# A gated Fourier and squared-ReLU mix in split float32: h as the transposed product, x's operands of three products from DRAM, and one more second-level product

## The chip, the cores and the metric

The kernel runs on one core of one Trainium2 chip. The metric is the device time of one execution in microseconds (us); of several runs the median is taken. The profile is a separate, profiled execution of the same program; it has a span (first to last instruction on the core) and a device time of its own.

## The reference, cut to what matters

```python
a = jnp.einsum("bsd,ed->bse", x, dft_hid_re)          # x is [2048, 1024]
b = jnp.einsum("bsd,ed->bse", x, dft_hid_im)
y = jnp.einsum("ts,bse->bte", dft_seq_re, a) - jnp.einsum("ts,bse->bte", dft_seq_im, b)
h = jnp.einsum("bsd,df->bsf", x, w1) + b1             # w1 is [1024, 3584]
r = jnp.where(h > 0, h, 0)
o = jnp.einsum("bsf,fd->bsd", r * r, w2) + b2
g = sigmoid((x * gate_w).sum(-1, keepdims=True))
out = g * y + (1 - g) * o
```

All of it is float32. x enters three times: in a and b, in h, and in the gate.

## The kernel before, in words

**Four stages.** x_stage (line 664) makes "x W", the products a and b, and keeps them in DRAM (`ab`). c_stage (780) makes y times g, kept in DRAM (`gy`). h_stage (683) makes the squared ReLU of h, kept in DRAM (`h_far`), in two parts: part 0 has 2048 of the 3584 features, part 1 the other 1536. o_stage (802) makes the output. On TensorE (PE) the stages stand one after the other, each a list of steps.

**Split float32.** An operand is a block of 128 partitions by 1024 floats. ScalarE (ACT) makes `hi`, its rounding to fp32r (line 220), and VectorE (DVE) makes `lo`, the difference (line 230). A step multiplies two operands by `hi*hi`, `hi*lo` and `lo*hi` (line 306): per 128 output rows six matmuls of 512 columns. A step has `rows` such rows: 4 in x_stage and in the first part of h, 3 in the second part, whose weight operands are 768 floats wide.

**Seven products.** Each stage is cut into 2x2 quarters and multiplied by seven products in place of eight (`seven`, line 366), in the order 1, 2, 5, 6, 3, 7, 4. The factors of a product are quarters, or sums S1 to S4 of left quarters and T1 to T4 of right quarters (lines 33 to 38):

```python
SUMS_L = {"S1": ((1, 0), (1, 1), ADD), "S2": ("S1", (0, 0), SUB), "S3": ((0, 0), (1, 0), SUB),
          "S4": ((0, 1), "S2", SUB)}
FACTORS = {1: ((0, 0), (0, 0)), 2: ((0, 1), (1, 0)), 3: ("S4", (1, 1)), 4: ((1, 1), "T4"), 5: ("S1", "T1"),
           6: ("S2", "T2"), 7: ("S3", "T3")}
```

The sums are DVE work on raw blocks from DRAM (line 172). In `wide` (line 568, for x_stage and h_stage) a product is made in one of two ways. `direct` (line 611) cuts it into 2x2 blocks and takes eight steps; its factors are four left and four right operands. `twice` (line 623) applies the seven products once more to those blocks: seven steps, with seven left and seven right operands and four further sums on each side. Which products go `twice` is in TWICE_X and TWICE_H (lines 20 and 24): x_stage and the first part have 1, 2, 5, 3 and 4, the second part 2, 5, 3 and 4. Products 6 and 7 are direct everywhere.

**Left and right.** In x_stage x is the left matrix (its sums are S1 to S4) and W the right one. In h_stage w1 is the left one and x the right one (sums T1 to T4), so the sums of x that h_stage needs are others than those of x_stage, and x_stage's operands cannot serve again.

**Taking the results up.** A step's result in PSUM goes to SBUF by an ACT copy (`put`, line 596) or a DVE addition (`add`, line 603); product 7 and others start from a value that ACT copies into PSUM (line 293). When a block of h is complete, `final` (line 697) does two Relu with the bias (L700) and one Square (L702) on ACT, and a store to DRAM on GpSimd's (POOL) queue follows. Blocks completed by a DVE addition have their `final` put off by LATER = 3 steps.

**What sets the order.** A planner written out by hand (lines 909 to 966) walks over the steps and, ahead of each, emits loads on SyncE's (SP) queue, then the stores that are due (on POOL's queue), then sums with `hi`, then `lo`. An item is loaded as early as 12 steps ahead if slots are free, its sum and its `hi` are made at least 3 steps ahead, its `lo` at least 2; with time left by the planner's own costs, up to 9. There are 55 slots of one block each. Each engine works through its own list in order. A step is 24 matmuls with 4 rows and 18 with 3.

## Time and profile before

| | us |
|---|---|
| median of 3 runs | 1891.17 (1890.40 to 1892.99) |
| the profiled execution | 1888.96 |
| its span | 1886.9 |

In the profile, busy times are of five engines: PE (matmuls; PEld are its weight loads), DVE, ACT, POOL and SP. `L306` is line 306 of the kernel, `ps<-hi,lo` a matmul into PSUM that reads a `hi` and a `lo`, `raw` a block loaded from DRAM, `sum` a sum of blocks, `h`, `u` and `ab` results and intermediate results. A wait is written as the waiting instruction, an arrow, and what it waited for. Granted clock was 0.999 of full speed. The 8244 matmuls of line 306 are shared out so: x_stage 1224, c_stage 2580, the first part of h 1224, its second part 936, o_stage 2280.

### The profile page before, as it was taken

Reading aid. Unit: us, or ns where it says so; the run is one execution under the profiler, and the core shown is the slowest. Engines: PE = TensorE matmul, PEld = TensorE weight load, DVE = VectorE, ACT = ScalarE, POOL = GpSimd, SP = SyncE. Lnnn points to the kernel's source line nnn. Section 1 sums busy time; section 2 is a strip of 40 time slices with the busy share of each in tenths; the row PEclk is TensorE's granted clock in tenths of the full one; section 3 lists DMA queues with packets and bytes.
Section 4 is the critical chain, followed back from the end, with each engine's and each line's share of the span. In section 5 each row is a group of like instructions: output and inputs, shape, how many; then the busy total and the mean of one; then the engine's idle time right before and its main releaser. Section 6 shows DMA issues by size and latency. Waiting matters only on the chain.

```text
span 1886.9 us, 21962 instructions
## 1 busy us (share of the span) xinstructions
PE 1876.6 (99%) x8288; PEld 1551.3 (82%) x8288; DVE 1610.3 (85%) x1543; ACT 1001.3 (53%) x1123; POOL 86.8 (5%) x161
## 2 busy tenths in 40 slices
PE   9999999999999999999999999999999999999998
PEld 7888888888888888888888888888888888888887
DVE  8997898599777998798896997989976997789882
ACT  6474564363343554455484797767954434264440
POOL 0000110000010000000000000000100001000000
PEclk9999999999999999999999999999999999999999
DMA  5732989339786489383551865628872887629971
GB/s 223 247 121 86 348 288 412 129 117 375 261 312 256 151 322 383 139 312 112 170 198 56 325 228 195 228 84 299 293 259 97 317 336 265 218 103 370 409 300 45
DMA packets 128425, 442.93 MB, mean 235 GB/s; under 512 B 14128, under 2 KB 23616, under 8 KB 128320
## 3 DMA queue, kind: packets, MB, share of 16 engines
q1 hardware_dynamic: 106416, 363.26, 53.0%
q0 software_dynamic: 21472, 77.61, 10.3%
q8 instruction: 65, 1.06, 0.2%
q10 hardware_dynamic: 432, 0.66, 0.1%
q14 instruction: 40, 0.33, 0.1%
HBM read 362.83 MB, written 78.65 MB: 234 GB/s over the span
## 4 chain that ended last, share of the span: by engine, by line
PE 97%; DVE 2%; ACT 0%; DMA 0%; issue 0%; SPq 0%; DVEq 0%; ACTq 0%
PE ps L306 97%; DVE lo L230 1%; DVE h L603 0%; DVE sum L172 0%; DMA raw<-in_w 0%; DVE o L818 0%; ACT u L596 0%; ACT hi L220 0%; DVE o L820 0%; DVE raw L172 0%; SPq L152 0%; DVEq L172 0%; DVEq L230 0%; ACTq L596 0%
## 5 line engine op out<-in xcount | busy, mean ns | idle before, releaser
L306 PE MATMUL ps<-hi 128*128 128x512 f32 x2328 | 905.7, 390 | 4.0 <-ACT hi L220 3.6
L306 PE MATMUL ps<-lo,hi 128*128 128x512 f32 x2328 | 905.3, 389 | 0.0
L306 PE MATMUL ps<-hi,lo 128*128 128x512 f32 x2328 | 904.2, 389 | 0.1
L220 ACT ACTIVATE hi<-raw 128x1024 fp32r<-128x1024 f32 (+2 forms) x413 | 420.6, 1037 | 399.0 <-DVE raw L172 274.1
L230 DVE TENSOR_TENSOR lo<-raw,hi 128x1024 fp32r<-128x1024 f32 (+2 forms) x413 | 484.5, 1199 | 57.5 <-ACT hi L220 31.3
L306 PEld LDWEIGHTS ps<-hi 128*128 128x128 f32 x2328 | 437.2, 188 | 95.9 <-ACT hi L220 4.2
L306 PEld LDWEIGHTS ps<-hi,lo 128*128 128x128 f32 x2328 | 437.1, 188 | 92.0 <-DVE lo L230 1.0
L306 PEld LDWEIGHTS ps<-lo,hi 128*128 128x128 f32 x2328 | 437.3, 188 | 91.0 <-DVE lo L230 0.4
L172 DVE TENSOR_TENSOR raw<-raw 128x1024 f32<-128x1024 f32 (+1 forms) x276 | 326.4, 1207 | 56.4 <-DMA raw<-in_ct 19.4
L220 ACT ACTIVATE hi<-sum 128x1024 fp32r<-128x1024 f32 (+1 forms) x172 | 176.1, 1036 | 184.8 <-DVE sum L172 151.2
L306 PE MATMUL ps<-hi,both 128*128 128x512 f32 x840 | 259.8, 389 | 0.0
L230 DVE TENSOR_TENSOR lo<-sum,hi 128x1024 fp32r<-128x1024 f32 (+1 forms) x172 | 203.3, 1198 | 32.9 <-PE ps L306 16.6
L306 PEld LDWEIGHTS ps<-hi,both 128*128 128x128 f32 x840 | 157.7, 188 | 33.8 <-ACT ps L293 0.7
L306 PE MATMUL ps<-lo,both 128*128 128x512 f32 x420 | 163.5, 389 | 0.0
L172 DVE TENSOR_TENSOR sum<-raw 128x1024 f32<-128x1024 f32 (+1 forms) x116 | 121.9, 1066 | 35.4 <-PE ps L306 28.1
L172 DVE TENSOR_TENSOR sum<-raw,sum 128x1024 f32<-128x1024 f32 (+2 forms) x87 | 96.8, 1119 | 12.0 <-PE ps L306 11.7
L603 DVE TENSOR_TENSOR h<-h,ps 128x1024 f32<-128x1024 f32 x92 | 98.2, 1086 | 9.6 <-ACT u L596 7.1
L596 ACT ACTIVATE u<-ps 128x1024 f32<-128x1024 f32 x76 | 71.9, 950 | 62.0 <-PE ps L306 54.3
L306 PEld LDWEIGHTS ps<-lo,both 128*128 128x128 f32 x420 | 78.8, 188 | 16.1
L293 ACT ACTIVATE ps<-u 128x1024 f32<-128x1024 f32 (+1 forms) x74 | 70.0, 953 | 22.2 <-DVE o L831 12.0
L700 ACT ACTIVATE h<-h,b1c 128x512 f32<-128x512 f32 x112 | 74.3, 712 | 6.3 <-DVE h L603 6.0
L220 ACT ACTIVATE both<-sum 128x512 fp32r<-128x512 f32 x60 | 37.1, 625 | 52.7 <-DVE sum L172 33.4
(61 smaller groups left out, 650.5 us busy)
## 6 DMA issues: line engine op xcount, KB each, us to landing
raw<-in_ct SPq DMA_DIRECT2D x151, 512.0 KB, 6.2
raw<-h SPq DMA_DIRECT2D x132, 512.0 KB, 7.3
raw<-in_x SPq DMA_DIRECT2D x107, 512.0 KB, 5.3
raw<-in_w SPq DMA_DIRECT2D x98, 512.0 KB, 6.3
raw<-ab SPq DMA_DIRECT2D x72, 512.0 KB, 6.8
h<-h POOLq DMA_DIRECT2D x48, 512.0 KB, 5.7
raw<-in_w1a SPq DMA_DIRECT2D x36, 512.0 KB, 5.0
ab<-ab POOLq DMA_DIRECT2D x32, 512.0 KB, 6.7
```

The source lines that it names most:

```text
L172: nc.vector.tensor_tensor(self.slot[:, k, c], src[0][:, k, c], src[1][:, k, c], op=self.op)
L220: nc.scalar.activation(self.hi[:, k, c], self.block.slot[:, k, c], AF.Copy)
L230: nc.vector.tensor_tensor(self.lo[:, k, c], self.block.slot[:, k, c], self.hi[:, k, c].bitcast(F32), op=SUB)
L293: nc.scalar.activation(t[:, :n, :], b.slot[:, at:at + n, :], AF.Copy, scale=self.sign)
L306: nc.tensor.matmul(self.ps[r // self.per][:, r % self.per, :], a[:, kk, r * P:(r + 1) * P], b[:, kk, :], start=self.at == 1 and kk + n == ...
L596: nc.scalar.activation(view(near.slot, k), view(ps, k), AF.Copy, scale=float(sign))
L603: nc.vector.tensor_tensor(view(near.slot, k), view((src or dst)[k].slot, k), view(ps, k), op=ADD if sign > 0 else SUB)
L700: nc.scalar.activation(dst.slot[:, k, :], (dst.slot if ps is None else ps)[:, k, :], AF.Relu, bias=b1c[:, tile0 + k:tile0 + k + 1])
```

## The change

It has three parts.

- **The transposed product in h_stage** (`flip`, FLIP = True). The product of w1 and x is formed as its transpose is: x takes the sums S1 to S4 and the weights take T1 to T4, and the factors of every product change sides (`turn`). The steps on PE keep their form: weights stationary, x moving.
- **x's operands from x_stage by DRAM** (KEEP_X). x's operands of products 6, 3 and 5 are now the same in x_stage and in both parts of h_stage: four of product 6 (direct), seven each of products 3 and 5. x_stage stores their `hi` and `lo` to DRAM after making them (`keep`, 36 stores on POOL's queue). h_stage loads them back as finished operands (`Fetched`: two loads on SP's queue into two slots, with no sum, no `hi` and no `lo` to make). Products 1, 2, 4 and 7 make their operands of x as before.
- **One more product by a second level.** Product 1 of the second part goes `twice`: seven steps of 18 matmuls in place of eight.

FAR_WIDE, which was empty, goes. The listing of the changed program has 8226 matmuls of line 306, 58 fewer tensor-tensor instructions on DVE (1418 for 1476), 26 fewer activations (1095 for 1121), 36 more DMA issues on POOL and 40 more on SP: 72 loads of kept operands, and 32 fewer of x.

```diff
-FAR_TALL, FAR_WIDE = ("T2",), ()
-TWICE_H = (1, 2, 5, 3, 4), (2, 5, 3, 4)
+FAR_TALL = "T2",
+ALL = *range(1, 8), *(("direct", m, q) for m in range(2) for q in range(2))
+KEEP_X, KEEP_H, FLIP = {6: ALL, 3: ALL, 5: ALL}, {}, True
+TWICE_H = (1, 2, 5, 3, 4), (1, 2, 5, 3, 4)
...
+        def keep(self):
+
+            self.far = Kept("hi"), Kept("lo")
+            self.uses += 2
...
             for k, c in self.cuts:
                 nc.scalar.activation(self.hi[:, k, c], self.block.slot[:, k, c], AF.Copy)
                 yield
+            if self.far:
+                stores.append((self.far[0], Copy(self, self.hi.bitcast(F32)), 0, 2))
...
             self.block.used()
+            if self.far:
+                stores.append((self.far[1], Copy(self, self.lo.bitcast(F32)), 0, 2))
...
+    class Copy:
+        def __init__(self, base, slot):
+            self.base, self.slot, self.uses = base, slot, 1
+
+        def used(self):
+            self.base.used()
+
+    class Fetched:
+        def __init__(self, far):
+            self.blocks, self.uses = far, 0
+
+        def room(self):
+            return 2
...
+        def load(self, engines):
+            self.hi, self.lo = take("hi", F32R), take("lo", F32R)
+            for b, t in zip(self.blocks, (self.hi, self.lo)):
+                assert b.done
+                next(engines).dma_start(t.bitcast(F32), b.at)
+
+        def sum(self):
+            return 0.0
+
+        def rest(self):
+            return 0.0
...
+        def turn(a, b):
+            return (b, a) if flip else (a, b)
...
+        def of_x(p, part, make):
+
+            if (p, part) in shared:
+                return Fetched(shared[p, part])
+            o = make()
+            if part in keep.get(p, ()):
+                o.keep()
+                shared[p, part] = o.far
+            return o
...
-            l, r = FACTORS[p]
-            mvs = [[right[q, c].operand(r) for q in range(2)] for c in range(2)]
+            l, r = turn(*FACTORS[p])
+
+            def st(m, q):
+                o = lambda: left[m, q].operand(l, rows * P)
+                return o() if x_right else of_x(p, ("direct", m, q), o)
+
+            def mv(q, c):
+                o = lambda: right[q, c].operand(r)
+                return of_x(p, ("direct", c, q), o) if x_right else o()
+
+            mvs = [[mv(q, c) for q in range(2)] for c in range(2)]
...
-                l_, r_ = FACTORS[p2]
-                step(l2.operand(l_, rows * P), r2.operand(r_), group)
+                l_, r_ = turn(*FACTORS[p2])
+                st, mv = lambda: l2.operand(l_, rows * P), lambda: r2.operand(r_)
+                if x_right:
+                    step(st(), of_x(p, p2, mv), group)
+                else:
+                    step(of_x(p, p2, st), mv(), group)
...
-             WIDE, TWICE_H[part], target, final)
+             WIDE, TWICE_H[part], target, final, flip=FLIP, keep=KEEP_H)
```

More of the change, by code (lines that the diff above doesn't have):

```diff
@@ L242, in used, with extra @@
                 give(*((self.hi, self.lo) if self.width > 256 else (self.both,)))
+    class Copy:
[8 more added lines that the diff above has]
+            return 2
+        def extra(self):
+            return 0
+        def load(self, engines):
[7 more added lines that the diff above has]
+            return 0.0
+        def used(self):
+            self.uses -= 1
+            if not self.uses:
+                give(self.hi, self.lo)
     class Half:
@@ L623, in twice, with takes @@
         def twice(p, old, new, ends, drop, sign):
-            l, r = FACTORS[p]
-            l2 = Sums(lambda m, q: left[m, q].of(l, rows * P), SUMS_L, True)
-            r2 = Sums(lambda q, c: right[q, c].of(r), SUMS_R, True)
-            def takes(first, m, c, ends=False):
+            l, r = turn(*FACTORS[p])
+            l2 = Sums(lambda a, b: left[turn(a, b)].of(l, rows * P), turn(SUMS_L, SUMS_R)[0], True)
+            r2 = Sums(lambda a, b: right[turn(a, b)].of(r), turn(SUMS_L, SUMS_R)[1], True)
+            def takes(first, a, b, ends=False):
+                m, c = turn(a, b)
                 def f(rp, ps):
@@ L675, in final @@
             stores.append((to[dst], dst, 0, 2))
[L677 removed]
+        wide(lambda i, j, m, q: x4[2 * i + m, j, q], lambda j, n, q, c: w4[n, c, j, q], 4, WIDE, TWICE_X, target, final, -1, True,
+             x_right=False, keep=KEEP_X)
     h_far = {(j, q, t): Kept(f"h{j}{q}{t}") for j in range(2) for q in range(7) for t in range(4)}
@@ L871, in need @@
         o = o.base if isinstance(o, (View, Half)) else o
-        if id(o) in seen or not isinstance(o, (Part, Operand, Gate, Row)):
+        if id(o) in seen or not isinstance(o, (Part, Operand, Fetched, Gate, Row)):
             return
```

22 lines of the change are left out of this document (12 added, 10 removed).

## The prediction, written before the changed kernel had run

> **What bounds the kernel now.** I read the page first, then who PE waits for, then PE in order of time around the waits, and last the busy times by stretch.
>
> ```profile
> span 1886.9 us, 21962 instructions
> PE 1876.6 (99%) x8288; PEld 1551.3 (82%) x8288; DVE 1610.3 (85%) x1543; ACT 1001.3 (53%) x1123; POOL 86.8 (5%) x161
> GB/s 223 247 121 86 348 288 412 129 117 375 261 312 256 151 322 383 139 312 112 170 198 56 325 228 195 228 84 299 293 259 97 317 336 265 218 103 370 409 300 45
> PE 97%; DVE 2%; ACT 0%; DMA 0%; issue 0%; SPq 0%; DVEq 0%; ACTq 0%
> ```
>
> The chain that ended last is PE for 97%. The waits of PE are few:
>
> ```profile
> PE ps L306 <- ACT hi L220: 3.6, 2, 2.9
> PE ps L306 <- ACT ps L293: 0.3, 1, 0.3
> ```
>
> The 3.6 us lie in the first 15 us, which the change leaves alone. The other wait stands in the timeline of PE; the first row below opens a stretch of 190 single matmul rows that the second row closes:
>
> ```profile
> 1255.01 0.39 PE L306 MATMUL ps<-hi,lo 128*128 128x512 f32 x1
> ...
> 1297.85 0.39 PE L306 MATMUL ps<-hi,lo 128*128 128x512 f32 x1
> 1298.56 1.02 PE L306 MATMUL ps<-hi 128*128 128x512 f32 x2 [0.33 <-ACT ps L293]
> 1299.42 0.63 PE L306 MATMUL ps<-lo,hi 128*128 128x512 f32 x2
> 1300.11 0.50 PE L306 MATMUL ps<-hi,lo 128*128 128x512 f32 x1
> 1300.44 0.39 PE L306 MATMUL ps<-hi 128*128 128x512 f32 x1
> ```
>
> From start to start a matmul takes (1297.85 - 1255.01) / 189 = 0.2267 us, so 8244 take 1869 of the 1886.9 us. Between 1297.85 and 1300.44 six matmuls take 2.59 us instead of 1.36: **1.23 us are lost there**, and this is the only stop that I found after the start. It is larger than the 0.3 us of the wait row, because the matmul at 1300.11 is late too. DVE shows why:
>
> ```profile
> 1297.95 2.10 DVE L230 TENSOR_TENSOR lo<-raw,hi 128x1024 fp32r<-128x1024 f32 x2
> ```
>
> The two `lo` end at 1300.05, and the matmul that reads `hi,lo` starts 0.06 us later. So in the second part of h DVE once came too late. Counting matmuls back from there (5676 stand before it) at 0.2267 us gives the bounds of the products; the rows are the first part's product 4, then the second part's 1, 2, 5, 6, 3 and 7:
>
> ```profile
> 1112.50:1150.50 38.00, 38.00 (x169) 31.47 (x168) 37.44 (x35) 33.89 (x43) 3.73 (x7) 1.00 0.69 241
> 1150.50:1183.00 32.50, 32.50 (x145) 26.91 (x144) 22.15 (x23) 18.85 (x24) 1.60 (x3) 1.00 0.39 135
> 1183.00:1212.00 29.00, 29.00 (x130) 24.01 (x129) 27.25 (x30) 17.46 (x24) 2.16 (x4) 1.00 0.53 183
> 1212.00:1240.50 28.50, 28.50 (x128) 23.59 (x126) 28.27 (x30) 23.20 (x31) 2.16 (x4) 1.00 0.69 248
> 1240.50:1273.00 32.50, 32.50 (x145) 26.92 (x144) 25.13 (x26) 18.98 (x24) 0.00 (x0) 1.00 0.19 65
> 1273.00:1303.00 30.00, 29.59 (x129) 23.67 (x128) 29.45 (x31) 18.81 (x25) 1.60 (x3) 1.00 0.66 232
> 1303.00:1335.50 32.50, 32.50 (x145) 26.92 (x144) 31.93 (x34) 32.50 (x47) 4.85 (x9) 1.00 0.98 363
> ```
>
> After the length come busy us of PE, PEld, DVE, ACT and POOL, the clock, the DMA share and GB/s. DVE is full in the second-level products (28.27 of 28.50 in product 5) and has air in direct product 1 (22.15 of 32.50).
>
> **The change, part by part.** Prices, from the groups of the two parts of h:
>
> ```profile
> L230 DVE TENSOR_TENSOR lo<-raw,hi 128x1024 fp32r<-128x1024 f32 x72 | 86.9, 1222 | 13.1 <-PE ps L306 11.8 <-ACT ps L293 0.7 <-ACT hi L220 0.6
> L230 DVE TENSOR_TENSOR lo<-raw,hi 128x768 fp32r<-128x768 f32 x24 | 22.9, 957 | 0.2
> L603 DVE TENSOR_TENSOR h<-h,ps 128x1024 f32<-128x1024 f32 x69 | 83.9, 1219 | 9.1 <-ACT u L596 6.6 <-PE ps L306 1.6
> L603 DVE TENSOR_TENSOR h<-h,ps 128x512 f32<-128x512 f32 x23 | 15.8, 686 | 0.6 <-ACT u L596 0.4
> L220 ACT ACTIVATE hi<-raw 128x1024 fp32r<-128x1024 f32 x73 | 75.9, 1052 | 17.9 <-PE ps L306 12.5 <-DVE raw L172 2.3 <-DMA raw<-in_x 1.6
> L220 ACT ACTIVATE hi<-raw 128x768 fp32r<-128x768 f32 x24 | 20.0, 838 | 5.6 <-DVE raw L172 2.6 <-DMA raw<-in_w1b 1.3 <-DVE sum L172 1.2
> L596 ACT ACTIVATE u<-ps 128x1024 f32<-128x1024 f32 x38 | 38.7, 1018 | 40.0 <-PE ps L306 40.0
> L596 ACT ACTIVATE u<-ps 128x512 f32<-128x512 f32 x12 | 7.1, 589 | 1.5 <-PE ps L306 1.4
> ```
>
> *PE.* Product 1 of the second part falls from 8 to 7 steps of 18 matmuls: 18 x 0.2267 = **4.08 us**. All of it is on the path, since PE is the path. The transposition alone changes no count on PE.
>
> The Trainium skill ("TensorE: Matmul & The Clock Gate", section "Back-to-back issue gap") gives about 131 ns per matmul of 512 columns in a sustained stream with weight loads. By that 18 matmuls would be worth 2.36 us as an estimate, and the change 3.6 us with the stop below; the 190 rows above, at 227 ns, do not agree; the measurement decides, and I give that price no chance.
>
> *DVE, taken away.* Fetched operands need no `lo`, and their sums are not made. Product 5 saves four first and four second sums and seven `lo` of x, 15 x 1.222 = 18.3 us. Product 3 saves seven `lo` and four second sums of x and four first sums of the weights, whose factor becomes a plain quarter: 18.3 us in the first part, 17.3 in the second. Product 6 saves four sums and four `lo` of x, 9.8 us. That is about 46 us in each part. It lies beside PE and is worth only the lost 1.23 us: in product 3 DVE needs about 41 us before (14 `lo`, 12 sums, 7 evictions of 1.22 + 0.69) and 24 after, against PE's 28.6, so what comes last there is PE itself. I take the whole **1.23 us**; the bounds are 0 and 1.23.
>
> *DVE and ACT, added.* Product 1 of the second part needs 7 x (0.957 + 1.222) for `lo`, 4 x (0.957 + 1.222) for sums and 2 x (1.219 + 0.686) for evictions = 27.8 us in place of 4 x (0.957 + 1.222) = 8.7. On ACT, 7 x (0.838 + 1.052) for `hi` and six evictions or preloads of 1.018 + 0.589 = 22.9 us in place of 7.6 + 6.4 = 14.0. PE gives 28.6 us. So it fits by itself, but its neighbours are full: product 4 of the first part needs 48.8 us of DVE (14 `lo`, 12 sums, 7 evictions of two 1.219) against 38.1, and product 2 needs 37.3 (27.8 and five more evictions of 1.905) against 28.6. The surplus over the three is 10.7 - 0.8 + 8.7 = **18.6 us**. What DVE has done ahead must cover it. In the kernel before, products 2, 5, 6 and 3 run up 8.7 + 7.9 - 7.6 + 12.5 = 21.5 us by the same sums, and that ended in a stop of 1.23: some 20.3 us were covered. As 18.6 is under 20.3, I take **0** here; the bounds are 0 and 10.4 (below). In this stretch POOL's stores and SP's slots wait on the same engines, but PE's next reader of them is products away.
>
> *POOL and SP.* The 36 stores fall in x_stage, most of them between 80 and 180 us, where SP's loads leave the DMA engines at 86 to 121 GB/s (third and fourth slice). From the groups and the DMA issues:
>
> ```profile
> L127 POOL DMA_DIRECT2D ab<-ab x32 | 17.2, 538 | 273.9 <-DVE ab L603 261.0 <-ACT ab L674 12.9
> raw<-h SPq DMA_DIRECT2D x132, 512.0 KB, 7.3
> raw<-in_x SPq DMA_DIRECT2D x107, 512.0 KB, 5.3
> ab<-ab POOLq DMA_DIRECT2D x32, 512.0 KB, 6.7
> ```
>
> They cost POOL 36 x 0.54 = 19 us of an engine 5% busy, and a slot stays held for 6.7 us after its `hi` or `lo` is made, while the step that reads it stands two steps (10.9 us) or more ahead: hidden, 0. If the cover went, each slot late by 6.7 us would delay one operand; the planner's three steps, 16 us, take that in.
>
> *The loads of h.* 72 come, 32 of x go. Worst is product 5 of the second part: 14 x 0.524 MB of x and 8 x 0.393 MB of weights, 10.5 MB, and about 3.1 MB of h stored, in 28.6 us: 475 GB/s asked for, where the best slice moved 412 and the stretch at a DMA share of 0.98 moved 363. At 363 the 13.6 MB take 37.5 us, 8.9 late. In the listing of the changed program a fetched operand's load waits for no matmul nearer than 90 to its first reader (20.4 us); less 7.3 for landing, 13.1 us stay. So 0; the bounds are 0 and 3.6.
>
> Sum: 4.08 + 1.23 = 5.3 us. The profiled execution of 1888.96 (span 1886.9 and 2.1 around it) becomes 1883.7. The median shown is 2.2 higher; the metric is the median, so I forecast 1891.17 - 5.3 = **1885.9**.
>
> **The rivals.**
>
> *DMA comes late.* If loads and stores together get only 300 GB/s (293 to 317 in several slices, which were perhaps not asked for more), product 5's 13.6 MB take 45.3 us, 16.7 late, 3.6 beyond the 13.1. Once, that is 1889.5, within 0.2%. It decides below 13.6 / (28.6 + 13.1) = 326 GB/s. Against it: 412 and 409 in slices, 363 in a stretch. The Trainium skill ("HBM Reference", section "Specifications (TRN2)") gives a core about 358 GB/s when both cores of a domain stream, and about 425 alone; both are above 326, and this is a one-core run.
>
> *Slower: the seam between the parts.* Before, DVE entered product 2 after a direct product with 10 us of air. Now it enters product 1 from product 4, itself short. If it comes with only the two steps' lead at which `lo` is due, 2 x 18 x 0.2267 = 8.2 us, then 18.6 - 8.2 = 10.4 us stop PE: 1896.3, slower by 0.27%. It decides at a lead of 9.5 us (18.6 less 5.3 less 3.8). With three steps' lead, 12.2 us, the loss is 6.4 and the time 1892.3. ACT's 22.9 us and the `final`s of product 4 (each two L700 and a L702) lie there as well. Against it: in product 4 before, DVE was at 37.44 of 38.00 and PE did not stop, and the light products 5, 6 and 3 ahead of it let DVE arrive early.
>
> *The stop stays or moves.* Without the 1.23 the time is 1887.1, just faster by over 0.2%.
>
> *The change does nothing.* Excluded: the listing has 18 matmuls fewer.
>
> **How the numbers follow.** Chances: forecast, with or without the small stop, 0.60; late DMA or a seam loss of 1.5 to 9 us, 0.27; seam beyond that, 0.13. Faster by over 0.2% (under 1887.4) 0.60, within 0.2% 0.27, slower 0.13; 0.2% is about what a measurement of this kernel can tell from no change. Range: the low end is the forecast less the 0.8 us by which the lowest run lies under the median and 1.1 for small delays that I did not find, 1884.0; the high end takes in late DMA and most of the seam with three steps' lead, 1892.0.
>
> **What would show it.** Right: 8226 matmuls of L306 at 0.2267, no stop near the second part's product 3, DVE well under full in products 5, 6 and 3 of both parts, PE's waits in h below 0.5 us. Wrong: matmuls between about 1112 and 1208 us that start late after `lo` or an ACT copy (seam), or after a DMA of `hi` or `lo` (loads); stops before 280 us (stores).

## The result, and the profile after

The changed kernel is slower: **1901.20 us** median of 6 runs (1898.74 to 1904.01) beside 1890.79 of 6 runs of the kernel before (1889.88 to 1892.99); ratio 1.0058, 95% interval 1.0048 to 1.0068. The forecast was 1885.9, faster, with a range up to 1892.0. The profiled execution took 1902.23 us, 13.3 longer than the one before.

Line numbers moved with the change: the matmul is now L356, `hi` L228, `lo` L240, sums L175, the DVE additions L672, the ACT copies out of PSUM L665 and into it L343, the Relu of `final` L785. Loads that SP issues are L155, those of kept operands L281.

From the page of the changed kernel, the totals and the chain that ended last:

```profile
span 1900.5 us, 22000 instructions
...
PE 1878.2 (99%) x8270; PEld 1550.2 (82%) x8270; DVE 1543.6 (81%) x1485; ACT 975.2 (51%) x1097; POOL 105.9 (6%) x197
...
PE 89%; DVE 5%; DMA 4%; ACT 2%; issue 1%; SPq 0%; DVEq 0%; ACTq 0%
```

DVE has 67 us less to do, and 18 matmuls are gone. But the chain, which was PE for 97%, now leaves PE for DVE and DMA in 9%. Who PE waits for (us in total, times, longest):

```profile
PE ps L356 <- DVE ab L672: 4.0, 1, 4.0
PE ps L356 <- DVE u L672: 3.8, 2, 2.5
PE ps L356 <- ACT hi L228: 3.2, 1, 3.2
PE ps L356 <- DVE h L672: 3.0, 3, 1.3
PE ps L356 <- ACT ps L343: 1.6, 1, 1.6
```

The `hi` row is the start, as before. The others are new, and all but one wait for additions on an engine that is less busy than before. So DVE is not full on average; it is late in places. Where, the busy times by stretch tell. The kernel before:

```profile
180.00:280.00 100.00, 100.00 (x443) 82.81 (x442) 93.79 (x86) 59.14 (x59) 10.65 (x20) 1.00 0.86 313
280.00:870.00 590.00, 590.00 (x2603) 488.07 (x2602) 504.37 (x499) 261.05 (x283) 18.14 (x34) 1.00 0.69 259
870.00:1150.00 280.00, 280.00 (x1237) 231.86 (x1236) 247.72 (x217) 201.19 (x230) 17.06 (x32) 1.00 0.54 194
1150.00:1380.00 230.00, 229.59 (x1010) 189.29 (x1010) 209.08 (x213) 174.67 (x228) 18.79 (x35) 1.00 0.62 226
```

The changed one, in the same stretches (the last third of x_stage; its end and c_stage; the first part of h; its second part):

```profile
180.00:280.00 100.00, 96.01 (x416) 78.98 (x416) 88.33 (x78) 56.30 (x56) 11.20 (x21) 0.98 0.83 317
280.00:870.00 590.00, 590.00 (x2603) 488.14 (x2602) 503.99 (x502) 263.98 (x287) 19.19 (x36) 1.00 0.69 260
870.00:1150.00 280.00, 277.78 (x1225) 229.19 (x1223) 201.17 (x175) 170.55 (x194) 15.46 (x29) 1.00 0.60 219
1150.00:1380.00 230.00, 223.79 (x975) 183.43 (x974) 181.21 (x191) 165.90 (x222) 18.75 (x35) 0.99 0.73 267
```

The count behind PE's busy time is the measure used from here on: at 0.2267 us from start to start, each matmul that a stretch has fewer is 0.2267 us lost. Lost are 27 between 180 and 280 us (6.1 us), none in the long stretch behind it, 12 in the first part of h (2.7), 35 in the second (7.9), and 5 before 180 us (785 for 790; 1.1; they lie in the first 60 us, where it has 256 and the kernels of this case, but for one, count from 251 to 262). These 79 are 17.9 us; less the 4.08 us of the 18 matmuls saved, 13.8 us should be added, and the spans differ by 13.6. **The 18 matmuls went as forecast; three stretches that were priced at 0 cost four times as much.** (A few records are missing in a trace, so a count means something from about 4 on.)

**Place one, 206 us, in x_stage.** PE and then DVE of the changed kernel, in order of time:

```profile
206.65 0.47 PE L356 MATMUL ps<-hi 128*128 128x512 f32 x1 [3.99 <-DVE ab L672]
...
208.34 0.63 PE L356 MATMUL ps<-hi,lo 128*128 128x512 f32 x1
208.77 0.63 PE L356 MATMUL ps<-hi 128*128 128x512 f32 x1
```

```profile
198.04 1.23 DVE L175 TENSOR_TENSOR raw<-raw 128x1024 f32<-128x1024 f32 x1 [1.36 <-DMA raw<-in_w]
199.18 1.22 DVE L240 TENSOR_TENSOR lo<-raw,hi 128x1024 fp32r<-128x1024 f32 x1
203.01 1.23 DVE L175 TENSOR_TENSOR raw<-raw 128x1024 f32<-128x1024 f32 x1 [2.61 <-DMA raw<-in_x]
204.16 1.22 DVE L240 TENSOR_TENSOR lo<-raw,hi 128x1024 fp32r<-128x1024 f32 x1
205.29 1.21 DVE L672 TENSOR_TENSOR ab<-ab,ps 128x1024 f32<-128x1024 f32 x1
```

DVE works through its list in order. It stood 1.36 + 2.61 = 3.97 us before two sums whose blocks had not landed, and the addition that PE needed was behind them; PE stood 3.99 us. The chain of waits has one load there, of x, that took 13.10 us from issue to landing. The rows from 208.34 on show a second loss: 0.43 us from start to start, about twice the normal time, for some 3 us.

**Place two, the seam and product 5 of the second part of h.** Stretches of the changed kernel, then rows of DVE and of PE, the first of each at the seam, the second in product 5:

```profile
1180.00:1210.00 30.00, 27.45 (x115) 22.20 (x114) 28.33 (x31) 12.58 (x16) 0.00 (x0) 0.94 0.41 136
1210.00:1240.00 30.00, 30.00 (x134) 24.64 (x132) 20.21 (x24) 22.66 (x33) 4.29 (x8) 1.00 1.00 377
1240.00:1270.00 30.00, 27.11 (x119) 21.92 (x118) 14.53 (x16) 16.11 (x21) 0.00 (x0) 1.00 0.62 234
```

```profile
1175.04 1.22 DVE L175 TENSOR_TENSOR sum<-sum,raw 128x1024 f32<-128x1024 f32 x1 [2.60 <-DMA raw<-in_x]
...
1237.99 0.96 DVE L175 TENSOR_TENSOR raw<-raw 128x768 f32<-128x768 f32 x1 [6.03 <-DMA raw<-in_w1b]
```

```profile
1190.07 0.55 PE L356 MATMUL ps<-hi 128*128 128x512 f32 x1 [2.55 <-DVE u L672]
...
1251.84 0.50 PE L356 MATMUL ps<-hi 128*128 128x512 f32 x1 [1.30 <-DVE h L672]
```

At the seam, where the second part of h begins, DVE is nearly full (28.33 of 30.00) and PE loses 19 of 134 matmuls. A late load has a share in that: DVE stood 2.60 us before a block of x that took 8.24 us from issue to landing, and worked from there without a gap up to the addition that PE stood 2.55 us for. In product 5 DVE is half idle (14.53 of 30.00) and PE still loses 15: there DVE waited 6.03 us for a block of weights, with the DMA engines full just before (share 1.00, 377 GB/s).

**Between them, the first part of h.** PE stops twice there, for 1.28 us at 917 and for 0.95 us at 954, each time for an addition of DVE. Rows of DVE and of PE at the first stop:

```profile
914.92 1.22 DVE L175 TENSOR_TENSOR raw<-raw 128x1024 f32<-128x1024 f32 x1 [3.05 <-DMA raw<-in_w1a]
```

```profile
917.33 0.50 PE L356 MATMUL ps<-hi 128*128 128x512 f32 x1 [1.28 <-DVE u L672]
```

It is the same picture: DVE stood before a sum whose block had not landed, 3.05 us here and 2.50 us, at 933, ahead of the second stop, and the addition was behind it.

### The profile page after: what moved, and what is told of

Its sections match the earlier page's. It is cut to its first block, busy times and chain, and to the rows that moved or that the text cites. A ratio compares the mean times of both kernels' runs of the same rounds, so it can differ in the third digit from the quotient of the medians.

```text
span 1900.5 us, 22000 instructions
## 1 busy us (share of the span) xinstructions
PE 1878.2 (99%) x8270; PEld 1550.2 (82%) x8270; DVE 1543.6 (81%) x1485; ACT 975.2 (51%) x1097; POOL 105.9 (6%) x197
## 4 chain that ended last, share of the span: by engine, by line
PE 89%; DVE 5%; DMA 4%; ACT 2%; issue 1%; SPq 0%; DVEq 0%; ACTq 0%
PE ps L356 89%; DMA raw<-in_x 1%; DVE lo L240 1%; DVE h L672 1%; DMA raw<-in_w1a 1%; DMA raw<-in_w1b 1%; DVE sum L175 1%; ACT h L785 0%; ACT hi L228 0%; ACT h L787 0%; DVE raw L175 0%; ACT u L665 0%; DVE u L672 0%; ACT ps L343 0%; SPq L155 0%
## 5 line engine op out<-in xcount | busy, mean ns | idle before, releaser
L356 PE MATMUL ps<-hi 128*128 128x512 f32 x2322 | 905.1, 390 | 15.7 <-DVE ab L672 4.0
L356 PE MATMUL ps<-lo,hi 128*128 128x512 f32 x2322 | 904.5, 390 | 0.0
L356 PE MATMUL ps<-hi,lo 128*128 128x512 f32 x2322 | 903.7, 390 | 0.4 <-DVE lo L240 0.4
L228 ACT ACTIVATE hi<-raw 128x1024 fp32r<-128x1024 f32 (+2 forms) x391 | 398.3, 1037 | 418.0 <-DVE raw L175 304.3
L356 PEld LDWEIGHTS ps<-hi 128*128 128x128 f32 x2322 | 436.7, 188 | 110.7 <-DVE u L672 4.7
L356 PEld LDWEIGHTS ps<-hi,lo 128*128 128x128 f32 x2322 | 437.0, 188 | 92.0 <-DVE lo L240 1.0
L356 PEld LDWEIGHTS ps<-lo,hi 128*128 128x128 f32 x2322 | 436.7, 188 | 91.1 <-DVE lo L240 0.3
L240 DVE TENSOR_TENSOR lo<-raw,hi 128x1024 fp32r<-128x1024 f32 (+2 forms) x391 | 457.6, 1194 | 60.5 <-ACT hi L228 39.7
L175 DVE TENSOR_TENSOR raw<-raw 128x1024 f32<-128x1024 f32 (+1 forms) x252 | 297.3, 1201 | 77.4 <-DMA raw<-in_w1a 17.4
L228 ACT ACTIVATE hi<-sum 128x1024 fp32r<-128x1024 f32 (+1 forms) x164 | 167.6, 1031 | 182.8 <-DVE sum L175 126.6
L356 PE MATMUL ps<-hi,both 128*128 128x512 f32 x840 | 259.7, 389 | 0.0
L240 DVE TENSOR_TENSOR lo<-sum,hi 128x1024 fp32r<-128x1024 f32 (+1 forms) x164 | 192.9, 1186 | 48.9 <-ACT hi L228 27.7
L356 PEld LDWEIGHTS ps<-hi,both 128*128 128x128 f32 x840 | 157.7, 188 | 33.6 <-ACT ps L343 0.8
L356 PE MATMUL ps<-lo,both 128*128 128x512 f32 x420 | 163.4, 389 | 0.0
L175 DVE TENSOR_TENSOR sum<-raw 128x1024 f32<-128x1024 f32 (+2 forms) x112 | 116.3, 1052 | 32.5 <-PE ps L356 21.8
L672 DVE TENSOR_TENSOR h<-h,ps 128x1024 f32<-128x1024 f32 x92 | 98.3, 1080 | 49.5 <-ACT u L665 41.1
L665 ACT ACTIVATE u<-ps 128x1024 f32<-128x1024 f32 x78 | 73.4, 947 | 76.4 <-PE ps L356 62.8
L175 DVE TENSOR_TENSOR sum<-raw,sum 128x1024 f32<-128x1024 f32 (+2 forms) x86 | 93.5, 1093 | 16.2 <-PE ps L356 14.6
L356 PEld LDWEIGHTS ps<-lo,both 128*128 128x128 f32 x420 | 78.8, 188 | 16.2
L343 ACT ACTIVATE ps<-u 128x1024 f32<-128x1024 f32 (+1 forms) x76 | 71.7, 950 | 23.6 <-DVE o L916 11.9
L785 ACT ACTIVATE h<-h,b1c 128x512 f32<-128x512 f32 x112 | 74.0, 712 | 14.2 <-DVE h L672 14.1
L228 ACT ACTIVATE both<-sum 128x512 fp32r<-128x512 f32 x60 | 37.1, 624 | 52.0 <-DVE sum L175 36.0
```

The costliest lines, as they stand in the source:

```text
L175: nc.vector.tensor_tensor(self.slot[:, k, c], src[0][:, k, c], src[1][:, k, c], op=self.op)
L228: nc.scalar.activation(self.hi[:, k, c], self.block.slot[:, k, c], AF.Copy)
L240: nc.vector.tensor_tensor(self.lo[:, k, c], self.block.slot[:, k, c], self.hi[:, k, c].bitcast(F32), op=SUB)
L343: nc.scalar.activation(t[:, :n, :], b.slot[:, at:at + n, :], AF.Copy, scale=self.sign)
L356: nc.tensor.matmul(self.ps[r // self.per][:, r % self.per, :], a[:, kk, r * P:(r + 1) * P], b[:, kk, :], start=self.at == 1 and kk + n == ...
L665: nc.scalar.activation(view(near.slot, k), view(ps, k), AF.Copy, scale=float(sign))
```

## The experiments

The theory after reading both traces: the loss has separate, local causes: the last kept stores in x_stage, DVE's surplus at the seam, and loads of h that come late. The main rivals were one cause for all (more traffic everywhere, a cost in proportion to it) and the transposition itself. Each run is compared with runs of the kernel before made together with it. The table has median, ratio with its interval, and matmuls in four stretches.

| kernel | us | ratio | 180:280 | 280:870 | 870:1150 | 1150:1380 |
|---|---|---|---|---|---|---|
| before | 1890 to 1891 | | 443 | 2603 | 1237 | 1010 |
| after | 1901.20 | 1.0058 [1.0048, 1.0068] | 416 | 2603 | 1225 | 975 |
| flip_only | 1893.16 | 1.0018 [1.0008, 1.0027] | 443 | 2603 | 1225 | 1011 |
| flip_keep | 1890.83 | 1.0001 [0.9991, 1.0010] | 443 | 2601 | 1236 | 1013 |
| stores_only | 1899.10 | 1.0051 [1.0036, 1.0066] | 419 | 2603 | 1221 | 1012 |
| keep_no3 | 1897.42 | 1.0040 [1.0025, 1.0055] | 443 | 2603 | 1219 | 977 |
| p1_only | 1891.75 | 1.0010 [1.0001, 1.0019] | 443 | 2603 | 1237 | 987 |
| keep_no_p1 | 1898.76 | 1.0049 [1.0032, 1.0066] | 414 | 2603 | 1231 | 1002 |
| late_none | 1893.77 | 1.0019 [1.0009, 1.0029] | 443 | 2603 | 1235 | 973 |
| late_2 | 1885.78 | 0.9978 [0.9968, 0.9988] | 443 | 2601 | 1237 | 1011 |
| late_1 | 1898.95 | 1.0049 [1.0034, 1.0064] | 443 | 2603 | 1237 | 960 |
| late_25 | 1893.46 | 1.0018 [1.0009, 1.0028] | 443 | 2603 | 1237 | 986 |
| late_25_hi | 1894.69 | 1.0021 [1.0012, 1.0031] | 443 | 2603 | 1235 | 976 |
| late_25_one | 1890.42 | 1.0005 [0.9995, 1.0015] | 442 | 2603 | 1235 | 989 |
| late_25_pool | 1903.26 | 1.0068 [1.0053, 1.0083] | 443 | 2603 | 1234 | 936 |
| late_25_keep | 1893.17 | 1.0016 [1.0006, 1.0025] | 443 | 2602 | 1237 | 975 |
| late_25_raws | 1904.48 | 1.0074 [1.0059, 1.0089] | 432 | 2591 | 1236 | 971 |
| after_raws6 | 1900.06 | 1.0054 [1.0039, 1.0069] | 413 | 2575 | 1234 | 1004 |
| after_keep | 1906.11 | 1.0082 [1.0065, 1.0099] | 413 | 2603 | 1223 | 966 |
| no3_h6 | 1897.71 | 1.0041 [1.0026, 1.0056] | 443 | 2603 | 1219 | 977 |

### The stop of x_stage: the last stores

*stores_only*: all 36 operands kept, none fetched, product 1 as before.

```diff
-TWICE_H = (1, 2, 5, 3, 4), (1, 2, 5, 3, 4)
+TWICE_H = (1, 2, 5, 3, 4), (2, 5, 3, 4)
...
-            if (p, part) in shared:
+            if False:
```

> Transposed; x_stage stores the 36 blocks, but h does not read them back and makes its operands as before; product 1 direct. Theory A: the loss in x_stage alone, a stop at about 206 us of 4 us with a slow clock after it, 6 to 8 us longer than before. Theory B, or a stop that came by chance in one execution: within 0.1% of before.

*keep_no3*: the changed kernel without the 14 stores (and the fetches) of product 3, the last that x_stage keeps.

```diff
-KEEP_X, KEEP_H, FLIP = {6: ALL, 3: ALL, 5: ALL}, {}, True
+KEEP_X, KEEP_H, FLIP = {6: ALL, 5: ALL}, {}, True
```

> The changed kernel with product 3 taken out of KEEP_X: x_stage stores 22 blocks instead of 36, none of them after about 145 us; product 3 makes its operands in h again, product 1 of the second part is still by a second level. Theory A (what costs in x_stage is the last stores, of product 3, which meet the loads of product 7 and the stores of ab where the DMA engines were full already): the stop at about 206 us goes, 32 matmuls lost before 280 us become 5 or fewer, and the time is 5 to 7 us shorter than the changed kernel's, 1.0020 to 1.0035 of before. Rival D (any store of an operand costs, by the slots it holds or by its descriptors, in proportion to the number): 22/36 of the loss stays, 20 matmuls, and the time is 2 to 3 us shorter than the changed kernel's.

With stores alone the stop is there (419), and DVE stands before the same two loads, 1.4 and 2.6 us; without product 3's stores it is gone (443 of 443), and not smaller in proportion. The times of both runs miss what was expected, since h moves as well: stores_only is 8.9 us slower than before, not 6 to 8 (it loses 16 matmuls in the first part), and keep_no3 is 3.8 us faster than the changed kernel, not 5 to 7 (h is no better than with product 3). The same stretch of time, busy times of the kernel before, of the changed one and of keep_no3:

```profile
200.00:204.00 4.00, 4.00 (x19) 3.32 (x18) 4.00 (x5) 1.25 (x2) 0.82 (x2) 1.00 1.03 421
```

```profile
200.00:204.00 4.00, 2.66 (x12) 1.88 (x10) 1.39 (x2) 1.28 (x2) 0.00 (x0) 1.00 1.03 421
```

```profile
200.00:204.00 4.00, 4.00 (x20) 3.30 (x19) 4.00 (x4) 2.33 (x3) 0.53 (x1) 1.00 1.02 417
```

The DMA engines are full in all three (share 1.02 and 1.03, 417 to 421 GB/s): full engines alone are not the stop. What the changed kernel adds here is four late stores of product 3, issued between 185 and 195 us, three before the late load of x and one while it was under way: 4 x 0.524 MB at 419 GB/s are, as an estimate, 5.0 us of all the engines' time, beside loads that DVE waited 3.97 us for. The median time to landing in 180 to 215 us rose from 6.7 to 9.1 us for blocks of x and from 8.0 to 11.3 for W. A rival is that the stores hold slots that the loads then wait for. Against it speaks when SP issues the two loads of x there, of which one is the late one, in the changed kernel and in keep_no3:

```profile
189.44 0.97 SPq L155 DMA_DIRECT2D raw<-in_x  x2
```

```profile
189.56 0.80 SPq L155 DMA_DIRECT2D raw<-in_x  x2
```

They were issued no later; the late one took longer to land. That it is the last four of the fourteen stores of product 3 is read from these times; no run leaves out the four alone.

### The transposition

*flip_only*: both parts of h transposed, nothing kept, product 1 as before.

```diff
-KEEP_X, KEEP_H, FLIP = {6: ALL, 3: ALL, 5: ALL}, {}, True
-TWICE_H = (1, 2, 5, 3, 4), (1, 2, 5, 3, 4)
+KEEP_X, KEEP_H, FLIP = {}, {}, True
+TWICE_H = (1, 2, 5, 3, 4), (2, 5, 3, 4)
```

> The transposed product alone: nothing kept, nothing fetched, second part's product 1 direct as before. Theory A (three places: the stores in x_stage cost about 7 us of PE, the loads of kept operands in h 6, the seam into product 1 about 6, against a gain of 5.3): the transposition costs nothing, ratio 1.000 +- 0.001, and the stop of 1.2 us in product 3 of the second part stays. Theory B (all of it is the seam): the same. Theory C (the transposition itself makes the order of DVE's work worse): slower by 3 us or more.

It costs 12 matmuls in the first part, with the same work on every engine. PE stops in one place; ACT and then DVE, 30 us earlier, show from where:

```profile
984.41 0.50 PE L356 MATMUL ps<-hi 128*128 128x512 f32 x1 [1.43 <-DVE h L672]
```

```profile
952.69 1.06 ACT L228 ACTIVATE hi<-raw 128x1024 fp32r<-128x1024 f32 x1 [2.08 <-DMA h<-h]
```

```profile
954.73 1.22 DVE L240 TENSOR_TENSOR lo<-sum,hi 128x1024 fp32r<-128x1024 f32 x1 [2.32 <-ACT hi L228]
```

ACT waited for a store out of the slot that it was to write, and DVE stood 2.32 us in a stretch where it is otherwise full to 984 us, where PE stopped for 1.43 and 0.39 us. Slots are handed out from a ring, the one longest free first; the planner keeps 5 free. *flip_keep* keeps 7:

```diff
-SLOTS, KEEP, RAWS = 55, 5, 4
+SLOTS, KEEP, RAWS = 55, 7, 4
```

> Both parts of h transposed, nothing kept, product 1 as before (that run: 1893.2 us, 12 matmuls lost between 870 and 1150 us), with the planner's reserve of free slots raised from 5 to 7, so that a slot rests longer in the ring before it is taken again. Theory (ScalarE's hi at 952.7 us waited 2.08 us for the store of h out of the slot it was to write; VectorE idled 2.32 us behind it in a stretch where it is full, and the two stops of 1.4 and 0.4 us at 984 and 988 us are that time): the wait goes, 1233 or more matmuls between 870 and 1150 us. Rival (the transposed order itself puts VectorE's evictions later): 1221 to 1229 there. The time can move by more than this, since the reserve holds in all stages: 1888 to 1896 us.

1236 of 1237: the wait for `h<-h` is gone, and so are the stops. The transposition is not costly in itself; it changed which slot met which store. So flip_only missed Theory A on both counts: the ratio is above 1.001, and the stop in product 3 did not stay.

The changed kernel loses 12 matmuls in the first part too, but that the numbers are equal is chance: no `hi` of ACT waits for `h<-h` there, and its stops are those at 917 and 954 us, behind late loads.

### The seam

*p1_only*: the kernel before with the one change in TWICE_H.

```diff
-TWICE_H = (1, 2, 5, 3, 4), (2, 5, 3, 4)
+TWICE_H = (1, 2, 5, 3, 4), (1, 2, 5, 3, 4)
```

> The kernel before with nothing but the second part's product 1 by a second level (no transposition, nothing kept). 18 matmuls fewer, 4.1 us. Theory A: DVE is short from the first part's product 4 on, without the relief of fetched operands, so PE stops in the second part for 5 to 14 us; the time is 1 to 10 us longer than before, and no stop stands in x_stage. Theory B: the seam costs 15 us or more by itself, so 10 us longer. If the second level were free: 4 us shorter.

*keep_no_p1*: the changed kernel with TWICE_H of before (the opposite edit).

> The change without its last part: transposed, operands of products 6, 3 and 5 kept and fetched, second part's product 1 direct. Theory A: x_stage loses about 7 us, the first part's product 2 about 3 and the second part's product 5 some 3, the old stop of 1.2 goes: 8 to 13 us longer than before. Theory B: no loss, 1.2 us shorter than before.

*late_2* and *late_none*: only the second part of h is transposed, with its product 1 by a second level. late_2 keeps product 2 of x_stage in place of 6, 3 and 5 and fetches it there; late_none keeps nothing.

```diff
-KEEP_X, KEEP_H, FLIP = {6: ALL, 3: ALL, 5: ALL}, {}, True
+KEEP_X, KEEP_H, FLIP = {2: ALL}, {}, True
...
-             keep={}):
+             keep={}, fetch=True):
...
-            if (p, part) in shared:
+            if fetch and (p, part) in shared:
...
-             WIDE, TWICE_H[part], target, final, flip=FLIP, keep=KEEP_H)
+             WIDE, TWICE_H[part], target, final, flip=bool(part), keep=KEEP_H, fetch=bool(part))
```

> As late_1, but x's operands of product 2 are kept (stores at about 45 to 90 us) and fetched by the second part. DVE needs 37.3 - 13.4 = 23.9 us in product 2 and 27.8 in product 1. Theory A: the seam's loss of 5 us falls to 0 to 2, and the time is 0.998 to 1.000 of before. If stores at any place of x_stage cost: over 1.001.

> Only the second part of h is transposed, its product 1 goes by a second level, and nothing is kept or fetched (correct output). It differs from the run that fetched product 2 alone (1885.8 us, no stop in the second part) by those fetches only. Theory (VectorE's surplus at the seam, 18.6 us in the prediction, is what stops TensorE; fetching product 2 took 18.3 us of it away): 15 to 30 matmuls are lost between 1150 and 1380 us (980 to 996 there in place of 1011), the time is 1889 to 1893 us. Rival (the transposed order by itself covers the seam, the fetches of product 2 do nothing): 1005 or more matmuls there, 1885 to 1887 us.

The second level alone (p1_only) costs 23 matmuls, 5.2 us, more than the 4.08 us that it saves; late_none loses 37, more than the 15 to 30 that were expected. The rows of p1_only, late_none and late_2 for 1180 to 1210 us:

```profile
1180.00:1210.00 30.00, 27.64 (x122) 22.59 (x121) 29.73 (x32) 17.83 (x24) 2.16 (x4) 1.00 0.60 198
```

```profile
1180.00:1210.00 30.00, 27.06 (x119) 22.11 (x118) 29.78 (x32) 16.22 (x22) 2.17 (x4) 0.98 0.58 192
```

```profile
1180.00:1210.00 30.00, 30.00 (x134) 24.84 (x133) 27.36 (x29) 17.14 (x24) 2.16 (x4) 1.00 0.76 271
```

In the first two DVE is full (29.7 of 30.0) and PE stops. PE's first stops there end waits for ACT's `hi` (2.36 us at 1207 in p1_only, 2.94 at 1209 in late_none), and ACT had stood 4.14 and 4.93 us (4.16 and 5.09) for DVE and then had the `final`s and `hi` of that time to make in one go: DVE's lateness reaches PE by way of ACT. In late_2 fetching product 2, whose factor of x is a plain quarter, takes four sums and seven `lo` of x from DVE, 11 x 1.222 = 13.4 us (not the 18.3 us that late_none's expectation has); the air is back (27.36) and PE does not stop, though the DMA engines carry 271 GB/s in place of 192. late_none loses 38 more than late_2, late_2 nothing beside the kernel before. So the second level at the seam makes a lack of DVE time: of the surplus of 18.6 us, what DVE had done ahead covered, as an estimate, some 13 (18.6 less the 5.2 of p1_only), and 13.4 us less work there cures it. The fetch takes seven `hi` from ACT as well (7.4 us at 1.052), so this pair of runs does not part DVE's time from ACT's. What helped is the fetch of a product **at** the seam, in one run of two that have it (late_1, below, loses). The change fetches products 5, 6 and 3, whose relief comes after it; at its own seam (1150 to 1210 us: 243 matmuls for 269) it loses 5.9 us, the late block of x among the causes. keep_no_p1, without the second level, loses 8 in the whole second part, and is 8.5 us slower than before, as expected.

late_2 beats both kernels: 1885.78 us, 0.9978 [0.9968, 0.9988].

### The loads of h

*late_1* and *late_25* are late_2 with `KEEP_X = {1: ALL}` and `{2: ALL, 5: ALL}`.

> Aimed at the seam: only the second part is transposed, only x's operands of product 1 are kept (14 stores, early in x_stage) and fetched, by the second part alone; product 1 of the second part by a second level. In product 1 DVE then needs 27.8 - 13.4 = 14.4 us in 28.6, so the surplus over the first part's product 4 and the second part's 1 and 2 falls from 18.6 to 5. Theory A: the seam loses nothing, the first part loses nothing, and 4.1 us less 0 to 2 us of start-up disturbance remain: 0.9975 to 0.9995 of before. If the seam is not DVE's time but the order of the steps: 1.000 to 1.002.

> As late_2, with product 5 kept as well (14 more stores, at about 82 to 125 us) and fetched by the second part. Theory A: as late_2, less the 1.2 us of the old stop in product 3, unless the fetches of product 2 and 5, one after the other at some 370 GB/s asked for, come late: 0.997 to 1.001 of before.

Both miss. late_1 fetches the product at the seam as well, yet loses 50 matmuls there, and 16 in the first 60 us of the run (244 for 260, where all the other kernels have 251 to 262), where its stores are issued. DVE of late_1 and of late_25 where PE stops:

```profile
1162.71 1.23 DVE L175 TENSOR_TENSOR sum<-raw 128x1024 f32<-128x1024 f32 x1 [5.66 <-DMA raw<-in_x]
1168.78 0.96 DVE L175 TENSOR_TENSOR sum<-raw 128x768 f32<-128x768 f32 x1 [4.84 <-DMA raw<-in_w1b]
```

```profile
1212.68 1.22 DVE L175 TENSOR_TENSOR raw<-raw 128x1024 f32<-128x1024 f32 x1 [4.82 <-DMA raw<-in_x]
1213.82 1.81 DVE L672 TENSOR_TENSOR h<-u,ps 128x1024 f32<-128x1024 f32 x2
```

It is the picture of x_stage again: an idle DVE before a sum whose block has not landed, and the additions that PE needs behind it (in late_25 PE stops at 1215.09 for 1.00 us, at 1241.19 for 2.05). PE waits for no fetched operand; the late ones are the raw blocks among them. Seven runs were to tell what makes them late. Five change late_25 in one respect:

```diff
# late_25_hi: same slots, half the bytes (the slot `held` is given back with hi)
-            self.hi, self.lo = take("hi", F32R), take("lo", F32R)
-            for b, t in zip(self.blocks, (self.hi, self.lo)):
+            self.hi, self.held = take("hi", F32R), take("lo", F32R)
+            self.lo = self.hi
+            for b, t in zip(self.blocks, (self.hi,)):
# late_25_one, on top of that: half the slots
+            self.hi = self.lo = take("hi", F32R)
# late_25_pool: GpSimd's queue
-                next(engines).dma_start(t.bitcast(F32), b.at)
+                nc.gpsimd.dma_start(t.bitcast(F32), b.at)
# late_25_raws: budget of blocks loaded ahead; late_25_keep: the reserve, as in flip_keep
-SLOTS, KEEP, RAWS = 55, 5, 4
+SLOTS, KEEP, RAWS = 55, 5, 6
```

> As the run that fetched products 2 and 5 in the second part (1893.5 us, 24 matmuls lost between 1150 and 1380 us), but each fetched operand loads its hi alone; the slot of its lo is held just as long and stays empty, and TensorE reads hi in its place. Left out: the lo half of the fetched operands, so 7 MB of loads less in the second part; slots, steps, matmuls and the order of SP's queue stay. Theory A (DMA engines: 394 to 410 GB/s there, loads of x land late, VectorE idles for 4.8 us): 1006 to 1011 matmuls between 1150 and 1380 us, 1885.5 to 1888 us. Theory B (slots held early by fetched operands make SP wait before the loads behind them): 980 to 992 matmuls, 1892 to 1895 us.

> As the run that fetched products 2 and 5 in the second part (1893.5 us, 24 matmuls lost between 1150 and 1380 us), with the fetched loads issued on GpSimd's queue in place of SP's. Same bytes, same slots. Theory C (SP issues in order: a fetched load that waits for its slot holds up the loads of x and w1b behind it): 1003 or more matmuls between 1150 and 1380 us, 1885.5 to 1888 us. Theory A (DMA engines are full, whichever queue issues): 975 to 995 matmuls, 1891 to 1896 us.

> As the run that fetched products 2 and 5 in the second part (1893.5 us, 24 matmuls lost between 1150 and 1380 us), with the planner's budget of blocks loaded ahead raised from 4 to 6. Theory D (a fetched operand counts two of four blocks until its step comes near, so the loads of x and w1b behind it are planned late, and VectorE idles for them): 1003 or more matmuls between 1150 and 1380 us. Rival E (slots: the ring is empty, SP waits for TensorE's reads whatever the budget): 975 to 995 there. The budget holds in all stages, so the time is judged in this stretch; 1884 to 1890 us by D, 1890 to 1897 by E.

> As the run that fetched products 2 and 5 in the second part (1893.5 us, 24 matmuls lost between 1150 and 1380 us), with the planner's reserve of free slots raised from 5 to 7. Theory E (fetched operands take their two slots at the load, so the ring runs empty and loads and hi wait for stores and reads of its last users): 1003 or more matmuls between 1150 and 1380 us, 1884 to 1890 us. Theory D (budget of blocks): 975 to 995 there, 1890 to 1897 us.

> As the run in which a fetched operand loads its hi alone and keeps an empty slot for its lo (1894.7 us, 976 matmuls between 1150 and 1380 us), without that empty slot: same loads, matmuls and steps. Left out: the lo half of the fetched operands. Slots as the cause (SP waits for TensorE to free a slot, x lands late, VectorE's queue stands behind the sum that waits for it): 1003 or more matmuls in that stretch, 1885 to 1888 us. Rival (the order that the planner gives, with its budget of four blocks, in which a fetched operand still counts two): 970 to 990, 1892 to 1896 us.

None brings the stretch back. Half the bytes leave DVE's first wait as it was, and only with half the slots as well does it shrink; the same sum in late_25_hi and late_25_one:

```profile
1213.69 1.23 DVE L175 TENSOR_TENSOR raw<-raw 128x1024 f32<-128x1024 f32 x1 [4.91 <-DMA raw<-in_x]
```

```profile
1212.33 1.23 DVE L175 TENSOR_TENSOR raw<-raw 128x1024 f32<-128x1024 f32 x1 [1.00 <-DMA raw<-in_x]
```

From late_25_hi to late_25_one 13 matmuls come back (976 to 989), so slots are part of it; 22 stay lost, with DVE waiting for x again and again (5.5 us in all between 1195 and 1260 us). GpSimd's queue and the larger budget make it worse (936 and 971), and the reserve leaves the time as it was (1893.17 for 1893.46, at 975 matmuls): the expectations that one of these limits is *the* cause all missed, and three of these runs lose more than either of their theories had.

The same two limits in the changed kernel itself (RAWS = 6; KEEP = 7):

> The changed kernel with the planner's budget of blocks loaded ahead raised from 4 to 6. Theory D (fetched operands fill the budget, the loads behind them are planned late): 1233 or more matmuls between 870 and 1150 us and 995 or more between 1150 and 1380, 1890 to 1896 us. Rival E (slots or transfers): 1215 to 1229 and 965 to 985, 1899 to 1906 us. x_stage can move either way: loads further ahead meet the stores earlier.

> The changed kernel with the reserve of free slots raised from 5 to 7. The stop of x_stage has its cause in the stores of product 3 meeting the loads on the DMA engines, so it stays by that theory: 408 to 425 matmuls between 180 and 280 us. The first part of h lost 12 matmuls (by transposition alone 12 too, which this reserve cured there): by the ring theory 1233 or more between 870 and 1150 us, by a theory of late transfers 1219 to 1229. Second part (35 lost): 990 or more by the ring theory, 970 to 985 otherwise. Time 1893 to 1897 us if h is cured, 1899 to 1903 if not.

And a sum of the account: keep_no3 with a budget of six in the steps of h alone, `h_at` to `o_at`:

```diff
-            if o.need > i + SUMS and o.room() + sum(e.room() for e in items[summed:loaded]) > RAWS:
+            if o.need > i + SUMS and o.room() + sum(e.room() for e in items[summed:loaded]) > (6 if h_at <= i < o_at else RAWS):
```

> The changed kernel without the keeping and fetching of product 3, and in the two parts of h alone a budget of six blocks loaded ahead in place of four. If the account of the runs so far holds (stores of product 3 make the stop of x_stage; in h the budget that fetched operands fill makes most of the loss): 443 matmuls between 180 and 280 us, 2603 between 280 and 870, 1231 or more between 870 and 1150, 1000 or more between 1150 and 1380, and 1885 to 1890 us. If the six-block budget helped only with product 3 fetched too, h stays at 1219 and 977 or so and the time at 1896 to 1899 us.

In after_raws6 h comes back nearly whole (1234 and 1004 for 1225 and 975, 8.6 us), but 28 more are lost at the end of x_stage (2575 for 2603; PE waits 1.55 us at 282 and 2.62 at 296), and the time stays at 1900.06. The reserve that cured flip_only does not help here (1223 and 966, 1906.11 us). And no3_h6 fails the account: x_stage is clean, but h stays at 1219 and 977, to the matmul that of keep_no3. A larger budget helps the one order and not the other.

**What stays open.** The waits of DVE between 1195 and 1260 us in late_25, for blocks from DRAM (total, times, longest):

```profile
DVE raw L175 <- DMA raw<-in_x: 5.0, 2, 4.8
DVE raw L175 <- DMA raw<-in_w1b: 2.3, 3, 1.5
```

Together 7.3 us; in its five variants they are 6.3 to 13.2 us, in the kernel before, in late_none and in late_2 there are none. That fetching product 5 behind product 2 brings them is shown; of bytes, slots, queue, reserve and budget, slots are shown to be a part (the slot itself, or the order that the planner gives with more of them free). SP's own waits between 1190 and 1214 us in late_25 narrow the rest:

```profile
SPq L155 <- DMA h<-h: 9.4, 2, 8.1
```

SP stood 8.1 us for a store of `h` out of the slot that it was to load into, and so issued the next blocks of x only from 1204.5 us on, for a sum that then began at 1212.68. The longest such wait is 6.5 to 9.5 us in four of the variants, and 5.4 us in late_25_one, where DVE's first wait fell to 1.00 us; it is 5.2 us in late_2, where DVE does not stand, and there is none in the kernel before and in late_none. In late_25_hi the DMA engines had a share of only 0.24 and 0.36 between 1195 and 1205 us: its late block was issued late, at 1207.7 us, and landed in 5.9. So the traces point at slots from which `h` is still being stored. No run takes that wait away, so it is not shown to be the cause.

## Why the prediction was wrong

- *18 matmuls, 4.08 us.* Right: 8270 for 8288 with the 44 of the start, at the same 0.2267 us.
- *The stop of 1.23 us at the second part's product 3 goes.* Right: no stop there in any kernel with product 3 fetched, and none in flip_only either, so the new order alone takes it away.
- *"They cost POOL 36 x 0.54 = 19 us ... hidden, 0."* **This step failed first**, by 6.1 us. It priced the engine that issues the stores and the slots that they hold, and placed them where the DMA engines had air, between 80 and 180 us. The last four fall behind 180 us, where the engines are full at 421 GB/s already in the kernel before; there the stores were paid for by the loads beside them. The prediction's own list of what would prove it wrong had these stops before 280 us, but no term for them.
- *The seam: "As 18.6 is under 20.3, I take 0."* **Failed**, by 5.9 us, inside its bounds of 0 to 10.4. The surplus of 18.6 was not measured by itself; the cover of 20.3 fails: with p1_only's loss of 5.2 us it was some 13 us. Those 20.3 had been inferred from products 2, 5, 6 and 3 of the kernel before, and no such lead stands ready at product 1, where p1_only has DVE full and PE standing. The rival with three steps' lead, 12.2 us, gave a loss of 6.4; it was the nearest to what was measured, partly by luck: it reckoned with DVE's work alone, and in the changed kernel a block of x that landed late has its share of the 5.9.
- *The loads of h: "So 0; the bounds are 0 and 3.6."* **Failed**: 15 matmuls, 3.4 us, in product 5 of the second part of the changed kernel and 12, 2.7 us, in its first part, together beyond the bound, as are the 5.4 us in late_25. The step asked whether a fetched operand comes in time for its reader. It does: no stop of PE in the changed kernel's h waits for one. It did not ask what its two loads do to the raw blocks beside them on the queue, in the slots and in the planner's budget.
- *"The transposition alone changes no count on PE."* True and not enough: flip_only loses 2.7 us in the first part by a wait for a slot. The changed kernel has other stops there.
- *DVE's 46 us less in each part.* Right in the first part (247.72 to 201.17 busy), and worth nothing there, since PE was the path.

Most of the loss is one habit: the new transfers were asked whether they themselves come in time, and not what they make late for an engine that takes its work in order.

## What to carry to other kernels

Before a transfer is called hidden, look up the DMA share in the very stretch where it falls, for its last instances above all, and name the loads behind it and who waits for them in order. Relief has to come before the place that lacks it: here one fetched product at the seam (late_2) gained 0.2%, where the change, with three fetched behind it, lost 0.6%; a fetch at the seam is no cure by itself (late_1 lost 0.5%). In a planned kernel a lead measured in one place is no stock that another can draw on.

## What the runs showed of the hardware

After some stops the matmuls start 0.43 us apart instead of 0.2267, with the granted clock near half. Behind the stop of 3.99 us in x_stage the rows of the changed kernel are (the clock is the third number from the end):

```profile
206.00:208.00 2.00, 1.35 (x5) 1.09 (x6) 2.00 (x3) 0.00 (x0) 0.53 (x1) 0.83 1.01 414
208.00:210.00 2.00, 2.00 (x6) 1.57 (x5) 2.00 (x3) 0.00 (x0) 0.53 (x1) 0.50 1.03 420
210.00:212.00 2.00, 2.00 (x9) 1.60 (x8) 1.77 (x2) 0.92 (x1) 0.00 (x0) 0.81 1.03 422
```

That is another 2 us or so. It followed a stop of 2.55 us as well (1190.07 in the changed kernel, 0.43 us for eight matmuls), one of 2.60 (late_1) and one of 2.94 (late_none), and in late_none two short stops of 1.11 and 0.58 us that began within 3 us of each other (clock 0.50 between 1244 and 1246 us); but not one of 2.87 us, in late_25_one:

```profile
1228.96 0.73 PE L356 MATMUL ps<-hi 128*128 128x512 f32 x2 [2.87 <-ACT ps L343]
1229.53 0.39 PE L356 MATMUL ps<-hi,lo 128*128 128x512 f32 x1
1229.76 0.62 PE L356 MATMUL ps<-hi 128*128 128x512 f32 x2
```

nor one of 2.05 (late_25). The Trainium skill ("TensorE: Matmul & The Clock Gate", section "Part 1: The HAM clock gate") says that the clock is halved after an idle window of about 3.4 us and that the window runs freely. The two speeds and the dependence on where a stop falls agree; that 2.55 us of standing were enough, and less in late_none, does not agree with a whole idle window.
